# Attention matmuls in contiguous bursts, w1's loads behind w3's, and one tile of softmax sums with a scaling on ScalarE

## The chip, the core and the metric

One Trainium2 chip, one of its cores. The metric is the device time of one launch in microseconds (us). Engines: PE is TensorE (PEld its weight loads), DVE is VectorE, ACT is ScalarE, POOL is GpSimd, SP is SyncE, which here only issues DMAs. Each engine works through its own instructions in the order in which they were built; where one waits, all behind it on that engine wait too.

## The reference

Three stages. An attention of 4 batches x 8 heads x 576 positions x 64 (pooled by four, plus a local one in a band of 7), a product of weight matrices with a gate by `(x@w1)*(x@w2)`, and a mixture of eight experts that picks one expert per token.

```python
q_d, k_d, v_d = (t.reshape(B, H, Sd, 4, D).mean(axis=3) for t in (q, k, v))
out_up = np.repeat(sm_attn(q_d, k_d, v_d), 4, axis=2)
scores = np.where(np.abs(pos[:, None] - pos[None, :]) < 4, scale * q @ k.T, -1e9)
attn = np.exp(scores - scores.max(-1)); attn /= attn.sum(-1) + 1e-9
x = out_up + attn @ v                     # 2304 tokens x 512
x = ((x @ w1) * (x @ w2)) @ w3 @ w_out    # 512 -> 1024 -> 1024 -> 512
e = argmax(x @ w_gate); gate = softmax(x @ w_gate)[e] * sigmoid((x @ w_output_gate)[e])
out = gate * (relu(x @ e_w1[e]) @ e_w2[e])
```

## The kernel before

The weights w_out, w3, w1 and w2 arrive as 64-bit floats in tiles of 128x512 (512 KB). DVE makes 32-bit floats of each by three integer operations (`f64_bits`, L127 to L129); ACT then splits off a high part in a rounded format (the "hi" cast) and POOL or DVE takes the rest (the "lo" part). A product of full precision is three matmuls, hi x hi, hi x lo, lo x hi (`mm3`, L390 to L392); these are called the large matmuls below.

The program runs, in this order: the gate phase (w_out is converted, transposed and multiplied with the two gate matrices, L318 and L322); WC, the product w3 @ w_out (384 large matmuls of 256 or 272 columns, tiles `w3T`); then for six groups of 384 tokens G1, the products with w1 and w2 (192 matmuls of 384 columns per group, `g1_step`), and G2, the product with WC (144 matmuls of 256 or 272 columns per group, `g2_step`), with the routing of each group in between; then the eight experts. w1 and w2 are converted (`w_part`, two tiles per step) during G1 of group 0, whose step f needs the tiles of f.

Attention is cut into 16 units (a batch and two heads). A unit has five parts: `a_T` (pools q and k), `a_S1` (24 local score matmuls of 32x64, L191, here **S**; 3 pooled score matmuls of 96x144, L202, **D**; maxima, exponentials), `a_S2` (sums, reciprocals, the two scalings, L219 to L225), `a_V1` (transposes: DVE's of the local weights, PE's of the pooled ones, L245, **pT**) and `a_V2` (4 pooled value matmuls of 64x144, L256, and 12 local ones of 64x96, L260, together **V**). S writes 32 of the array's columns and V 64, by a position in the array; D, pT and the large matmuls are not placed so. The five parts of successive units are put between the steps of WC and G1 by tables of step numbers, under `tc.high_priority(offset=120)`: a list scheduler then sets the order on each engine by priorities, so that attention and large matmuls mix. Group g of G1 needs the units of its tokens: units 0 to 3 for group 0, 4 to 7 for group 1, and so on.

PSUM has eight banks: two each in `ps1` (tag g1) and `ps2` (tag g2), three in `psa` (attention and routing), one in `psc` (the temporary `cv` of `f64_bits`). SP issues all loads in one order; a load waits there until its buffer is free.

Of the kernel before, what the change touches and what calls it, by code (L numbers as in the profile page):

```python
# [48 lines left out]
def attention_moe_kernel(ctx: ExitStack, tc: tile.TileContext, q, k, vw_in, v4_in, w1, w2, w3, w_out,  # L49
# [52 lines left out]

    staged = {}

    def pieces(m, n):
        return (slice(0, 256), slice(256, 512)) if (m, n) == ("o", 0) else (slice(0, 512),)

    def f64_load(m, n):
        if m == "o":
            t = mt([P, 512], I64, "f64w", tag=f"W{n}")  # L110
            src = w_out[P * n:P * n + P, :]
        elif m == "3":
            t = mt([P, 512], I64, "f64w", tag=f"W{8 + n % 4}")
# [70 lines left out]
    def a_S1(u):  # L184
# [3 lines left out]
        sl = ps[:, 0:384].rearrange("p (b h k) -> p b h k", b=6, h=2)  # L188
        for g in range(24):
            b, j = divmod(g, 4)  # L190
            nc.tensor.matmul(sl[32 * j:32 * j + 32, b], qT[:, 24 * g:24 * g + 32], kz[:, :, 24 * g:24 * g + 32],  # L191
                             start=True, stop=True, tile_position=(0, 32 * j))
        sm = at([P, 6, 2, 32], F32, "sm", bufs=2)
# [6 lines left out]
        qf = qz.rearrange("p h n -> p (h n)")  # L200
        for qb in range(3):
            nc.tensor.matmul(sd[:, qb], qf[:, 96 * qb:96 * qb + 96], d["kd"], start=True, stop=True)  # L202
# [9 lines left out]
        d.update(sm=sm, ed=ed, zd=zd)  # L212

    def a_S2(u):
        d = st[u]
        sm, ed = d["sm"], d["ed"]
        su = at([P, 6, 2], F32, "su", bufs=2)
        sd = d["zd"]
        nc.vector.tensor_reduce(out=su, in_=sm, axis=AX.X, op=ALU.add)  # L219
        nc.vector.tensor_scalar(su, su, 1e-9, None, op0=ALU.add)  # L220
        nc.vector.reciprocal(su, su)
        nc.gpsimd.tensor_tensor(sm, sm, su.unsqueeze(3).to_broadcast([P, 6, 2, 32]), op=ALU.mult)
        nc.vector.tensor_scalar(sd, sd, 4.0, 4e-9, op0=ALU.mult, op1=ALU.add)
        nc.vector.reciprocal(sd, sd)
        nc.gpsimd.tensor_tensor(ed, ed, sd.unsqueeze(2).to_broadcast([96, 3, 144]), op=ALU.mult)  # L225
        v4 = d["v4"]
        vd = at([72, 2, 2, D], F32, "vd", bufs=2)
        vt = v4[:, :, 0:2]
        nc.gpsimd.tensor_tensor(vt, vt, v4[:, :, 2:4], op=ALU.add)
        nc.gpsimd.tensor_tensor(vd.rearrange("p k h d -> p k (h d)"), vt[:, :, 0], vt[:, :, 1], op=ALU.add)  # L230
        d.update(vd=vd)

    def a_V1(u):
# [8 lines left out]
        for kb in range(2):  # L242
            pv = psa.tile([P, 512], F32, name="at", tag="at")
            for qb in range(3):
                nc.tensor.transpose(pv[0:72, 96 * qb:96 * qb + 96], ed[:, qb, 72 * kb:72 * kb + 72], ident[0:96, 0:96])  # L245
            nc.scalar.copy(out=pt[:, kb], in_=pv[0:72, 0:288])
        d["pt"] = pt

    def a_V2(u):
# [3 lines left out]
        xl = [psa.tile([P, 512], F32, name="at", tag="at") for _ in range(2)]  # L253
        for kb in range(2):
            for h in range(2):
                nc.tensor.matmul(xl[0][64 * h:64 * h + 64, 288:432], vd[:, kb, h, :], pt[:, kb, 144 * h:144 * h + 144],  # L256
                                 start=(kb == 0), stop=(kb == 1))
        for c in range(6):
            for h in range(2):
                nc.tensor.matmul(xl[c // 3][64 * h:64 * h + 64, 96 * (c % 3):96 * (c % 3) + 96], vw[:, c, D * h:D * h + D],  # L260
                                 bd[:, 2 * c + h, :], start=True, stop=True)
        up = at([P, 144], F32, "up")
        nc.scalar.copy(out=up, in_=xl[0][:, 288:432])
        for a in range(2):
# [42 lines left out]
    def gate_step(f, gps, src):  # L307
        t = mt([P, DM], F32, "wf", tag=f"W{12 + f % 4}")
        for c in pieces("o", f):
            f64_bits(src[:, c], t[:, c].bitcast(U32))  # L310
        w = mt([P, NW + HN[1]], F32R, "wo", tag=f"h{f}")
# [47 lines left out]
    def w_part(m, f):  # L359
# [516 lines left out]
    for n in range(KF):  # L876
        if n == 1:
            nc.sync.dma_start(out=wg[:, :, 0:E], in_=w_gate.rearrange("(k p) e -> p k e", p=P))
            nc.sync.dma_start(out=wg[:, :, E:2 * E], in_=w_ogate.rearrange("(k p) e -> p k e", p=P))
        f64_load("o", n)  # L880
# [165 lines left out]
def _laid_out(inputs):  # L1046
# [51 lines left out]
```

## Time and profile before

| | |
|---|---|
| time, median of 3 runs | 777.54 us (775.76 to 778.25) |
| the profiled execution's own time | 771.75 us |
| its span, first to last instruction | 769.9 us |
| busy: PE, DVE, POOL, ACT | 96%, 57%, 42%, 36% |
| mean granted TensorE clock | 0.989 of full |

The profiled execution ended 5.8 us before the median of the timed runs, so differences are worked out on the profile and carried over to the median. A row of the timeline has the start in us, the length in us, the engine, the line, the operation, out<-in, the shapes and how many were merged; fp32 matmuls appear twice (x8 is four matmuls). The end of a matmul is modelled and includes the pipeline, so the time that one takes is read from start to start.

### The profile page before, as it was taken

What the parts mean: (1) busy time and instruction counts of PE and PEld (TensorE: products, weight loads), DVE (VectorE), ACT (ScalarE), POOL (GpSimd) and SP (SyncE); (2) the same over time, 40 slices, a digit from 0 to 9 for tenths busy, and PEclk for the clock granted to TensorE, in tenths of its full rate; (3) what the DMA queues carried; (4) which work ended last, traced back from release to release, by engine and by line L of the source; (5) the groups of instructions that cost most, each with busy time, mean ns of one, the idle gap of its engine ahead of it and who ended that gap; (6) DMA issues with size and microseconds to landing.
All of it is one profiled execution on the core that took longest, in us unless ns stands there. A gap on an engine that the chain in (4) does not pass through costs nothing.

```text
span 769.9 us, 14699 instructions
## 1 busy us (share of the span) xinstructions
PE 739.4 (96%) x5710; PEld 683.3 (89%) x5711; DVE 436.3 (57%) x940; ACT 279.6 (36%) x624; POOL 322.9 (42%) x306
## 2 busy tenths in 40 slices
PE   5789999999999999999999999989999999999995
PEld 3667987888978898899899999978999999999994
DVE  8977897962653254445324343455765566676731
ACT  3423534550233223323421212045443644544610
POOL 6744576852360125213201112035654656755611
PEclk9899999999999999999999999998999999999999
DMA  9994565542131313121110010256645447447301
GB/s 325 332 240 139 173 189 160 171 136 91 54 109 31 115 29 111 47 77 38 42 42 22 1 42 1 60 199 241 213 146 210 148 149 268 146 148 260 111 23 39
DMA packets 38264, 97.72 MB, mean 127 GB/s; under 512 B 6018, under 2 KB 12930, under 8 KB 38192
## 3 DMA queue, kind: packets, MB, share of 16 engines
q1 hardware_dynamic: 34768, 86.82, 35.1%
q0 software_dynamic: 3424, 9.93, 3.6%
q8 instruction: 46, 0.75, 0.4%
q14 instruction: 26, 0.21, 0.1%
HBM read 84.93 MB, written 12.29 MB: 126 GB/s over the span
## 4 chain that ended last, share of the span: by engine, by line
PE 86%; issue 5%; POOL 3%; DVE 3%; DMA 1%; ACT 1%; SPq 0%; POOLq 0%; ACTq 0%
PE g L390 24%; PE g L392 24%; PE g L391 23%; PE at L260 3%; PE at L191 3%; PE at L256 2%; PE at L202 2%; PE tr L686 1%; PE at L245 1%; PE tr L779 1%; POOL out_dram L769 1%; DMA early<-in_moe_w_dram 1%; PE g L322 1%; POOL W L713 1%; DVE wf L129 1%
## 5 line engine op out<-in xcount | busy, mean ns | idle before, releaser
L390 PE MATMUL g<-xh,W 128*128 128x384 f32 x384 | 133.8, 349 | 0.0
L392 PE MATMUL g<-xh,W 128*128 128x384 f32 x384 | 131.0, 342 | 0.0
L391 PE MATMUL g<-xl,W 128*128 128x384 f32 x384 | 130.8, 341 | 0.0
L713 DVE TENSOR_TENSOR W<-raw,W 128x1024 fp32r<-128x1024 f32 x32 | 87.9, 2780 | 32.2 <-ACT W L711 30.1
L713 POOL TENSOR_TENSOR W<-raw,W 128x1024 fp32r<-128x1024 f32 x29 | 82.8, 2879 | 37.0 <-ACT W L711 37.0
L390 PE MATMUL g<-xT,W 128*128 128x288 f32 (+6 forms) x256 | 82.2, 321 | 1.0 <-ACT xT L690 1.0
L391 PE MATMUL g<-xT,W 128*128 128x288 f32 (+6 forms) x256 | 80.2, 313 | 0.0
L392 PE MATMUL g<-xT,W 128*128 128x288 f32 (+6 forms) x256 | 80.0, 312 | 0.0
L423 POOL TENSOR_TENSOR h<-a,h 128x384 fp32r<-128x384 f32 x30 | 30.7, 1023 | 113.9 <-ACT h L421 113.7
L390 PEld LDWEIGHTS g<-xh,W 128*128 128x128 f32 x384 | 72.2, 188 | 3.2 <-issue 0.4
L392 PEld LDWEIGHTS g<-xh,W 128*128 128x128 f32 x384 | 72.1, 188 | 1.9 <-issue 0.4
L391 PEld LDWEIGHTS g<-xl,W 128*128 128x128 f32 x384 | 72.2, 188 | 1.5 <-issue 0.2
L390 PE MATMUL g<-wc,h 128*128 128x272 f32 (+1 forms) x240 | 70.2, 293 | 0.0
L391 PE MATMUL g<-wc,h 128*128 128x272 f32 (+1 forms) x240 | 70.0, 292 | 0.0
L390 PE MATMUL g<-h,W 128*128 128x288 f32 (+5 forms) x224 | 70.0, 312 | 0.0
L392 PE MATMUL g<-wc,h 128*128 128x272 f32 (+1 forms) x240 | 69.9, 292 | 0.0
L391 PE MATMUL g<-h,W 128*128 128x288 f32 (+5 forms) x224 | 68.1, 304 | 0.0
L392 PE MATMUL g<-h,W 128*128 128x288 f32 (+5 forms) x224 | 68.1, 304 | 0.0
L711 ACT CAST W<-raw 128x1024 fp32r<-128x1024 f32 x61 | 59.8, 1046 | 8.1 <-DMA raw<-in_moe_w_dram 4.3
L419 DVE TENSOR_TENSOR a<-g,a 128x384 f32<-128x384 f32 x48 | 26.7, 556 | 60.2 <-PE g L392 56.4
L739 ACT ACTIVATE h<-g 128x288 fp32r<-128x288 f32 (+6 forms) x64 | 27.9, 436 | 78.6 <-PE g L392 76.3
L390 PEld LDWEIGHTS g<-xT,W 128*128 128x128 f32 x256 | 49.1, 192 | 1.5 <-ACT xT L690 1.4
(255 smaller groups left out, 1721.8 us busy)
## 6 DMA issues: line engine op xcount, KB each, us to landing
raw<-in_moe_w_dram SPq DMA_DIRECT2D x61, 512.0 KB, 3.6
f64w<-in_moe_w_dram SPq DMA_DIRECT2D x16, 512.0 KB
f<-in_moe_w_dram SPq DMA_DIRECT2D x16, 512.0 KB, 6.5
vw<-in_vw_dram SPq DMA_DIRECT2D x16, 384.0 KB, 3.2
kc<-in_k_dram SPq DMA_DIRECT2D x16, 288.0 KB, 6.4
qT<-in_q_dram SPq DMA_DIRECT2D x16, 288.0 KB, 4.3
kz<-in_k_dram SPq DMA_DIRECT2D x32, 144.0 KB, 3.7
v<-in_v_dram SPq DMA_DIRECT2D x16, 288.0 KB
```

The source lines that it names most:

```text
L191: nc.tensor.matmul(sl[32 * j:32 * j + 32, b], qT[:, 24 * g:24 * g + 32], kz[:, :, 24 * g:24 * g + 32], start=True, stop=True, tile_positio ...
L202: nc.tensor.matmul(sd[:, qb], qf[:, 96 * qb:96 * qb + 96], d["kd"], start=True, stop=True)
L256: nc.tensor.matmul(xl[0][64 * h:64 * h + 64, 288:432], vd[:, kb, h, :], pt[:, kb, 144 * h:144 * h + 144], start=(kb == 0), stop=(kb == 1))
L260: nc.tensor.matmul(xl[c // 3][64 * h:64 * h + 64, 96 * (c % 3):96 * (c % 3) + 96], vw[:, c, D * h:D * h + D], bd[:, 2 * c + h, :], start=T ...
L390: nc.tensor.matmul(ps, whi, xhi, start=first, stop=False)
L391: nc.tensor.matmul(ps, whi, xlo, start=False, stop=False)
L392: return nc.tensor.matmul(ps, wlo, xhi, start=False, stop=last)
L419: nc.vector.tensor_tensor(a, pp[1][:, 0:G], a, op=ALU.mult)
L423: eng.tensor_tensor(lo, a, hi.bitcast(F32), op=ALU.subtract)
L711: nc.scalar.copy(out=hi, in_=t)
L713: ins = eng.tensor_tensor(lo, t, hi.bitcast(F32), op=ALU.subtract)
L739: return nc.scalar.activation(out=t[:, 0, 0:C], in_=ps[:, 0:C], func=AF.Relu), nc.vector.scalar_tensor_tensor(t[:, 1, 0:C], ps[:, 0:C], 0. ...
```

## The change

Six edits. (1) The PE instructions of S, D, pT and V are issued under a priority raised by a further 600, so that the scheduler puts them as soon as it counts their inputs as there, and together. (2) `psa` has four banks; `psc` is gone, and `cv` takes a bank of g1 (w_out and w3) or of g2 (w1 and w2). (3) The first four loads of w1 and w2 come behind the last load of w3 on SP. (4) Both softmaxes' sums lie in one tile of 128x15, with one addition of 1e-9 and one reciprocal for both; the factor 4 of the pooled one goes into the copy of V's result (0.25). (5) The pooled weights are scaled by three operations of ACT rather than one of POOL. (6) The two gate matrices are laid out in one row per partition by the host.

```diff
-    psa = actx.enter_context(tc.tile_pool(name="psa", bufs=3, space=PSUM))
-    psc = actx.enter_context(tc.tile_pool(name="psc", bufs=1, space=PSUM))
+    psa = actx.enter_context(tc.tile_pool(name="psa", bufs=4, space=PSUM))
...
-    def f64_bits(t, dst):
+    def f64_bits(t, dst, ps, tag):
...
-        c = psc.tile([P, 512], F32, name="cv", tag="cv").bitcast(U32)[:, 0:dst.shape[-1]]
+        c = ps.tile([P, 512], F32, name=tag, tag=tag).bitcast(U32)[:, 0:dst.shape[-1]]
...
+    sums = [at([P, 15], F32, f"sum{i}") for i in range(2)]
+    for t in sums:
+        nc.vector.memset(t, 1.0)
...
+    def burst():
+
+        return tc.high_priority(offset=600)
...
+        with burst():
+            for g in range(24):
+                b, j = divmod(g, 4)
+                nc.tensor.matmul(sl[32 * j:32 * j + 32, b], qT[:, 24 * g:24 * g + 32], kz[:, :, 24 * g:24 * g + 32],
+                                 start=True, stop=True, tile_position=(0, 32 * j))
...
-        zd = at([96, 3], F32, "zd", bufs=2)
+        zd = sums[u % 2][0:96, 12:15]
...
-        su = at([P, 6, 2], F32, "su", bufs=2)
-        sd = d["zd"]
+        sums_u = sums[u % 2]
+        su = sums_u[:, 0:12].rearrange("p (b h) -> p b h", b=6)
         nc.vector.tensor_reduce(out=su, in_=sm, axis=AX.X, op=ALU.add)
-        nc.vector.tensor_scalar(su, su, 1e-9, None, op0=ALU.add)
-        nc.vector.reciprocal(su, su)
+        nc.vector.tensor_scalar(sums_u, sums_u, 1e-9, None, op0=ALU.add)
+        nc.vector.reciprocal(sums_u, sums_u)
         nc.gpsimd.tensor_tensor(sm, sm, su.unsqueeze(3).to_broadcast([P, 6, 2, 32]), op=ALU.mult)
-        nc.vector.tensor_scalar(sd, sd, 4.0, 4e-9, op0=ALU.mult, op1=ALU.add)
-        nc.vector.reciprocal(sd, sd)
-        nc.gpsimd.tensor_tensor(ed, ed, sd.unsqueeze(2).to_broadcast([96, 3, 144]), op=ALU.mult)
+        for qb in range(3):
+            nc.scalar.activation(out=ed[:, qb], in_=ed[:, qb], func=AF.Copy, scale=sums_u[0:96, 12 + qb:13 + qb])
...
-        nc.scalar.copy(out=up, in_=xl[0][:, 288:432])
+        nc.scalar.mul(up, xl[0][:, 288:432], 0.25)
...
         if i == KF - 2:
-            ahead()
+            with tc.issue_after(f64_last[0].ins):
+                ahead()
```

The D, pT and V matmuls are put under `burst()` in the same way. How that moves the instructions shows at three places. The first is PE in G1 of group 1, where unit 8's V stands (`vd`, `vw` the values, `pt`, `bd` the weights, `xh`, `xl`, `W` the large matmuls'). Before:

```order
L391 MATMUL g1_2772<-xl_2382,W2_1618 128x384
L256 MATMUL at_2975<-pt_2759,vd_2630 64x144
L392 MATMUL g1_2772<-xh_2381,W6_1619 128x384
L256 MATMUL at_2975<-pt_2759,vd_2630 64x144
L390 MATMUL g1_2772<-xh_2381,W2_1618 128x384
L256 MATMUL at_2975<-pt_2759,vd_2630 64x144
L391 MATMUL g1_2772<-xl_2382,W2_1618 128x384
L256 MATMUL at_2975<-pt_2759,vd_2630 64x144
L392 MATMUL g1_2772<-xh_2381,W6_1619 128x384
```

And now (S and D of unit 10 just ahead of it):

```order
L199 MATMUL at_2828<-kz_108,qT0_109 32x64 x6
L211 MATMUL at_2858<-kd_2730,qz_112 96x144 x3
L199 MATMUL at_2828<-kz_108,qT0_109 32x64 x18
L266 MATMUL at_2955<-pt_2741,vd_2613 64x144 x4
L270 MATMUL at_2955<-bd_111,vw_2752 64x96 x6
L270 MATMUL at_2956<-bd_111,vw_2752 64x96 x6
L400 MATMUL g1_2796<-xh_2366,W3_1787 128x384
```

V's 16 matmuls, one by one between large ones before, stand in one piece; D has moved into the middle of S.

The second place is DVE around the end of WC (`f_...` are the loaded tiles of w1 and w2, `wc<-g` takes a finished half of WC out of its bank). Before:

```order
L355 TENSOR_TENSOR wc<-g_1065,wc 128x256
L127 TENSOR_SCALAR cv<-f_1138 128x512
L128 SCALAR_TENSOR_TENSOR cv<-f_1138,cv 128x512
L271 TENSOR_TENSOR xr<-at,up 128x288 x2
L129 SCALAR_TENSOR_TENSOR wf<-f_1138,cv 128x512
L127 TENSOR_SCALAR cv<-f_1140 128x512
```

Now:

```order
L365 TENSOR_TENSOR wc<-g_1295,wc 128x272
L127 TENSOR_SCALAR g_1352<-f_1132 128x512
L128 SCALAR_TENSOR_TENSOR g_1352<-f_1132,g_1352 128x512
L281 TENSOR_TENSOR xr<-at,up 128x192
L281 TENSOR_TENSOR xr<-at,up 128x96
L129 SCALAR_TENSOR_TENSOR wf<-f_1132,g_1352 128x512
```

The first tile of w1 was converted behind the sixth half of WC from the end (g_1065 is followed by five more), and is now converted behind the last but one (g_1295).

The third is SP, behind the first two loads of w3. Before:

```order
L169 DMA vw<-in_vw_dram 128x768
L119 DMA f_1138<-in_moe_w_dram 128x512
L119 DMA f_1140<-in_moe_w_dram 128x512
L119 DMA f_1142<-in_moe_w_dram 128x512
L153 DMA kc<-in_k_dram 128x576
L160 DMA kz<-in_k_dram 64x576 x2
```

Now:

```order
L176 DMA vw<-in_vw_dram 128x768
L160 DMA kc<-in_k_dram 128x576
L167 DMA kz<-in_k_dram 64x576 x2
L161 DMA qT_109<-in_q_dram 128x576
L160 DMA kc<-in_k_dram 128x576
L171 DMA v_549<-in_v_dram 72x1024
```

The loads of w1 and w2 have left this place; k and q of the next units stand there.

## Rows read from the trace of the kernel before

**Rows 1.** The page's first lines: span, then busy time of each engine.

```profile
span 769.9 us, 14699 instructions
```

**Rows 2.** Windows: stretch and its length, busy time by engine, clock, DMA share, GB/s.

```profile
0.00:28.70 28.70, 17.43 (x153) 12.69 (x154) 25.76 (x58) 12.45 (x27) 20.83 (x42) 1.00 0.94 335
28.70:101.10 72.40, 67.10 (x634) 57.67 (x638) 59.13 (x129) 30.82 (x83) 36.82 (x43) 0.95 0.71 202
101.10:168.20 67.10, 65.82 (x599) 56.27 (x598) 56.18 (x111) 33.03 (x88) 48.67 (x50) 1.00 0.55 167
168.20:242.30 74.10, 74.10 (x615) 63.73 (x614) 32.24 (x97) 21.72 (x62) 24.91 (x32) 1.00 0.26 78
242.30:318.20 75.90, 75.90 (x624) 66.61 (x623) 32.70 (x102) 24.14 (x67) 24.15 (x30) 1.00 0.27 79
318.20:400.00 81.80, 81.80 (x668) 76.39 (x667) 33.33 (x100) 25.32 (x68) 15.42 (x18) 1.00 0.14 42
```

**Rows 3.** Timeline of PE, 220 to 232 us: V between large matmuls one by one.

```profile
221.00 0.46 PE L256 MATMUL at<-pt,vd 72*64 72x144 f32 x2
221.39 0.45 PE L392 MATMUL g<-xh,W 128*128 128x384 f32 x1
...
231.47 0.34 PE L392 MATMUL g<-xh,W 128*128 128x384 f32 x1
```

**Rows 4.** Timeline of PE, 285 to 291 us: V in one piece, and pT.

```profile
285.27 0.71 PE L256 MATMUL at<-pt,vd 72*64 72x144 f32 x8
285.81 1.16 PE L260 MATMUL at<-bd,vw 128*64 128x96 f32 x24
...
287.19 0.34 PE L391 MATMUL g<-xl,W 128*128 128x384 f32 x1
287.36 0.34 PE L392 MATMUL g<-xh,W 128*128 128x384 f32 x1
...
290.46 0.66 PE L245 MATMUL at<-ident,ed 96*72 96x96 f32 x6
```

**Rows 5.** Timeline of PE, 218 to 221 us: S and D in one piece.

```profile
218.41 0.88 PE L191 MATMUL at<-kz,qT 128*32 128x64 f32 x48
219.21 0.98 PE L202 MATMUL at<-kd,qz 128*96 128x144 f32 x6
...
220.20 0.34 PE L391 MATMUL g<-xl,W 128*128 128x384 f32 x1
```

**Rows 6.** PE's groups by form, 168.2 to 400 us: xcount | busy us, mean ns.

```profile
L390 PE MATMUL g<-xh,W 128*128 128x384 f32 x200 | 70.2, 351 | 0.0
...
L390 PE MATMUL g<-wc,h 128*128 128x272 f32 x88 | 26.4, 300 | 0.0
...
L390 PE MATMUL g<-wc,h 128*128 128x256 f32 x82 | 24.0, 292 | 0.0
```

**Rows 7.** Groups of instructions, 0 to 168.2 us: the small operations of the softmaxes.

```profile
L210 ACT ACTIVATE ed<-at,md 96x144 f32<-96x144 f32 x24 | 8.8, 372 | 8.7 <-DVE md L206 8.7
...
L225 POOL TENSOR_TENSOR ed<-ed,zd 96x432 f32<-96x432 f32 x8 | 7.9, 993 | 4.2 <-DVE zd L224 4.2
...
L210 ACT ACTIVATION_READ_ACCUMULATOR ed<-at,md 96x1 f32 x24 | 4.7, 196 | 0.0
...
L223 DVE TENSOR_SCALAR zd<-zd 96x3 f32<-96x3 f32 x8 | 2.3, 289 | 0.0
...
L224 DVE RECIPROCAL zd<-zd 96x3 f32<-96x3 f32 x8 | 1.2, 156 | 0.0
```

**Rows 8.** Timeline of DVE, 96 to 99 us, and of PE, 116 us.

```profile
97.96 0.68 DVE L129 SCALAR_TENSOR_TENSOR wf<-f,cv 128x512 uint32<-128x512 uint32 x1
...
116.13 0.29 PE L392 MATMUL g<-wo,w3T 128*128 128x272 f32 x1
```

**Rows 9.** Timeline of PE, 50 us, and of POOL, 62 us: unit 2's D and its scaling.

```profile
50.09 0.41 PE L202 MATMUL at<-kd,qz 128*96 128x144 f32 x2
...
62.28 1.62 POOL L225 TENSOR_TENSOR ed<-ed,zd 96x432 f32<-96x432 f32 x1 [0.95 <-DVE zd L224]
```

More of the change, by code (lines that the diff above doesn't have):

```diff
@@ L103, in attention_moe_kernel @@
     staged = {}
+    f64_last = [None]
     def pieces(m, n):
@@ L188, in a_S1 @@
         sl = ps[:, 0:384].rearrange("p (b h k) -> p b h k", b=6, h=2)
[L189 to L192, printed above, removed]
+        with burst():
[3 more added lines that the diff above has]
+                                 start=True, stop=True, tile_position=(0, 32 * j))
         sm = at([P, 6, 2, 32], F32, "sm", bufs=2)
@@ L200, in a_S1 @@
         qf = qz.rearrange("p h n -> p (h n)")
-        for qb in range(3):
-            nc.tensor.matmul(sd[:, qb], qf[:, 96 * qb:96 * qb + 96], d["kd"], start=True, stop=True)
+        with burst():
+            for qb in range(3):
+                nc.tensor.matmul(sd[:, qb], qf[:, 96 * qb:96 * qb + 96], d["kd"], start=True, stop=True)
         ed = at([96, 3, 144], F32, "ed", bufs=2)
@@ L211, in a_S1 @@
                                  bias=md[:, qb:qb + 1], accum_out=zd[:, qb:qb + 1])
-        d.update(sm=sm, ed=ed, zd=zd)
+        d.update(sm=sm, ed=ed)
     def a_S2(u):
@@ L216, in a_S2 @@
         sm, ed = d["sm"], d["ed"]
-        su = at([P, 6, 2], F32, "su", bufs=2)
-        sd = d["zd"]
+        sums_u = sums[u % 2]
+        su = sums_u[:, 0:12].rearrange("p (b h) -> p b h", b=6)
         nc.vector.tensor_reduce(out=su, in_=sm, axis=AX.X, op=ALU.add)
-        nc.vector.tensor_scalar(su, su, 1e-9, None, op0=ALU.add)
-        nc.vector.reciprocal(su, su)
+        nc.vector.tensor_scalar(sums_u, sums_u, 1e-9, None, op0=ALU.add)
+        nc.vector.reciprocal(sums_u, sums_u)
         nc.gpsimd.tensor_tensor(sm, sm, su.unsqueeze(3).to_broadcast([P, 6, 2, 32]), op=ALU.mult)
-        nc.vector.tensor_scalar(sd, sd, 4.0, 4e-9, op0=ALU.mult, op1=ALU.add)
-        nc.vector.reciprocal(sd, sd)
-        nc.gpsimd.tensor_tensor(ed, ed, sd.unsqueeze(2).to_broadcast([96, 3, 144]), op=ALU.mult)
+        for qb in range(3):
+            nc.scalar.activation(out=ed[:, qb], in_=ed[:, qb], func=AF.Copy, scale=sums_u[0:96, 12 + qb:13 + qb])
         v4 = d["v4"]
@@ L243, in a_V1 @@
             pv = psa.tile([P, 512], F32, name="at", tag="at")
-            for qb in range(3):
-                nc.tensor.transpose(pv[0:72, 96 * qb:96 * qb + 96], ed[:, qb, 72 * kb:72 * kb + 72], ident[0:96, 0:96])
+            with burst():
+                for qb in range(3):
+                    nc.tensor.transpose(pv[0:72, 96 * qb:96 * qb + 96], ed[:, qb, 72 * kb:72 * kb + 72], ident[0:96, 0:96])
             nc.scalar.copy(out=pt[:, kb], in_=pv[0:72, 0:288])
@@ L253, in a_V2 @@
         xl = [psa.tile([P, 512], F32, name="at", tag="at") for _ in range(2)]
[L254 to L261, printed above, removed]
+        with burst():
+            for kb in range(2):
+                for h in range(2):
+                    nc.tensor.matmul(xl[0][64 * h:64 * h + 64, 288:432], vd[:, kb, h, :], pt[:, kb, 144 * h:144 * h + 144],
+                                     start=(kb == 0), stop=(kb == 1))
+            for c in range(6):
+                for h in range(2):
+                    nc.tensor.matmul(xl[c // 3][64 * h:64 * h + 64, 96 * (c % 3):96 * (c % 3) + 96], vw[:, c, D * h:D * h + D],
+                                     bd[:, 2 * c + h, :], start=True, stop=True)
         up = at([P, 144], F32, "up")
-        nc.scalar.copy(out=up, in_=xl[0][:, 288:432])
+        nc.scalar.mul(up, xl[0][:, 288:432], 0.25)
         for a in range(2):
@@ L877, in attention_moe_kernel @@
         if n == 1:
-            nc.sync.dma_start(out=wg[:, :, 0:E], in_=w_gate.rearrange("(k p) e -> p k e", p=P))
-            nc.sync.dma_start(out=wg[:, :, E:2 * E], in_=w_ogate.rearrange("(k p) e -> p k e", p=P))
+            nc.sync.dma_start(out=wg[:, :, 0:E], in_=w_gate.rearrange("p (k e) -> p k e", e=E))
+            nc.sync.dma_start(out=wg[:, :, E:2 * E], in_=w_ogate.rearrange("p (k e) -> p k e", e=E))
         f64_load("o", n)
@@ L1066, in _laid_out @@
         a[n] = _np.asarray(a[n]).reshape(KD, P, KF, P).transpose(2, 1, 0, 3).reshape(KF, P, 512)
+    for n in ("moe2_w_gate", "moe2_w_output_gate"):
+        a[n] = _np.asarray(a[n]).reshape(KD, P, E).transpose(1, 0, 2).reshape(P, KD * E)
     w = _np.asarray(a["moe2_w1"])
```

8 lines of the change are left out of this document (4 added, 4 removed).

## The prediction

> **What bounds the kernel now.** I read the page's head first, for the span [rows 1], then a table of windows by stage [rows 2], then the timeline of PE where attention mixes with large matmuls [rows 3 to 5]. The reader is to see two things in the windows. From 168.2 us on, PE is busy to the full (74.1 of 74.1, 75.9 of 75.9, 81.8 of 81.8) while DVE is at 32 to 33 us in each: here PE alone sets the end, and its time is a sum of what stands in its queue. Up to 168.2 us (the end of G1 of group 0) it is close: PE is busy 65.8 to 67.1 us of its stretches, but DVE is too, 25.76 of 28.7, 59.13 of 72.4 and 56.18 of 67.1, together 141.1 of 168.2 us. Every tile of w_out, w3, w1 and w2 passes through DVE there. So an edit on PE's queue is worth its full price behind 168.2 us, and before it only as far as DVE lets it.
>
> PE's "busy" hides a loss, and rows 3 and 4 show it. Two large matmuls of 384 columns in a row start 0.17 us apart (287.19 and 287.36 [rows 4]). One V in a single piece runs from 285.27 to 287.19, by when one large matmul (286.91 to 287.19) has run too: 1.92 less 0.17 is 1.75 us. The V that is mixed in one by one runs from 221.00 to 231.47, 10.47 us, with 15 large matmuls in it, which are worth 15 x 0.174 = 2.6 us: 7.86 us for the same V. Each of the 15 changes to and fro thus costs (7.86 - 1.75) / 15 = 0.41 us.
>
> **What the change does, part by part.** *Bursts behind 168.2 us.* First the floor of 168.2 to 400 us, 231.8 us long [rows 2]. Large matmuls: 3 x 200 of 384 columns, 3 x 88 of 272 and 3 x 82 of 256 [rows 6]. At 0.174 us, and in proportion to the columns 0.123 and 0.116 (an estimate), that is 104.4 + 32.5 + 28.5 = 165.4 us. Attention in single pieces: nine V at 1.75 = 15.8; eight S with D at 1.62 (218.41 to 220.20, less one large matmul [rows 5]) = 13.0; eight and a half pT at 0.66 at most [rows 4] = 5.6. The routing's 24 small matmuls I put at 2.5. The sum is 202.3, so 29.5 us are lost to changes. In the built order of before, PE goes 83 times from something else to S or V in this stretch, where 17 pieces (nine V, eight S with D) would need 17: 66 too many at 0.41 is 27 us, so count and loss agree.
>
> In the order of the changed kernel it goes there 31 times, for 16 pieces. The 15 beyond that are nearly all S again behind D: D now stands inside S (the first order fence). Before, no S stands right behind a D, so the price of that has no row. From below it is nothing, from above 0.41, as for a large matmul; I take 0.41, since a D uses the array unplaced, as a large matmul does. 15 x 0.41 = 6.2. The gain is 29.5 - 6.2 = 23.3; and one V (1.75) has moved ahead of 168.2, so this stretch gets shorter by 25.0. I take off 1.5 for places where a burst comes before its inputs do: **23.5 us**.
>
> A rule speaks against edit (1) here. The Trainium skill (TensorEngine Tiling (Array Packing), Key Properties) says that a change of tiling mode, not of tile alone, drains the engine. By that rule a burst with D in it is not one piece, as the 15 are counted above; a count of pieces alone, which lets them go free, would give 29.7 in place of 23.5. Rows 3 agree with the rule where large matmuls stand between; no row of before shows it for D inside S.
>
> *Up to the end of G1 of group 0.* The same work as before stands here, with V of the eighth unit in addition. PE's floor: in 28.7 to 168.2 us WC and G1 are 384 matmuls at about 0.12 and 192 at 0.174, 46 + 33 = 79 us. With five S and D, seven V and seven pT (8.1 + 12.3 + 4.6) and twelve changes too many (4.9) that is 109 us, and with two S, D and one V and pT that now stand ahead of WC (5.7) PE could end at 28.7 + 5.7 + 109 = 143 us. DVE's floor: edit (4) takes away 289 and 156 ns for eight units [rows 7], 3.6 us, so 137.5 us remain. In the busiest stretch of rows 2, the first, it is at 0.90; at that share it needs 153 us, at the 0.84 of the whole, 164. Two things hold it back. The 1e-9 is now added to both sums at once, so DVE waits for the pooled exponentials too, three of 372 + 196 ns on ACT [rows 7], 1.7 us per unit, and the conversions behind it wait along. And `cv` of w1 and w2 needs a bank of g2: four tiles had been converted when WC ended (the first at 97.96, WC's last matmul at 116.13 [rows 8]), now two; two tiles at 3 x 0.68 are 4 us behind WC, where G1 of group 0 waits for DVE with each step. I take 160 us for the end of this stage: **8 us** gained. Between the ends it can be 20 gained (148) or 4 lost (172).
>
> *Loads of w1 and w2 behind w3.* The first stretch moves 335 GB/s at a DMA share of 0.94 [rows 2], so 3 or 4 loads of 512 KB out of it bring k, q and w3 forward by some 1.5 us each. That comes off waits of DVE and is within the 8 us; w1's first tile is converted only at 96 to 99 us [rows 8]. If they came late, G1 of group 0 would wait for the first of them, at most the same 1.5 us each.
>
> *Edits with one answer.* The scaling moves from POOL (993 ns per unit [rows 7]) to ACT. The trace has no such operation; an ACT operation of this shape takes 372 ns, so three are 1.1 us, from nothing (where ACT waits anyway) to 1.7. ACT is busy 76 of the first 168.2 us and 22 to 25 in each later stretch [rows 2], so it hides there; if its queue is full, pT comes later by that much. It waits on the reciprocal, and w3's hi casts are queued behind it: that is in the range of the first stage. The fourth bank, 0.25 in the copy and the gate's layout cost and bring nothing that a row shows; the waits that a lack of a bank would have caused are covered by large matmuls, and would show as PE's idle time if that cover went.
>
> *Sum.* 8 + 23.5 = 31.5 us off the profiled execution's 771.75, to 740.25. Behind 400 us the order is the same and PE-bound or a chain behind PE, so it moves forward as a whole. The median of the runs is 777.54, 5.8 above the profiled one: the forecast for the median is **746.0 us**.
>
> **Rivals.** (a) *The first stage gives it back.* DVE's new wait for ACT costs eight times 1.7 = 13.6 us, and WC's end shifts 4: the stage ends at 172. For it: DVE is the second engine here, and its queue is in order. Against: the waits lie partly on work that is idle anyway. -4 + 23.5 = 19.5 gained: 758. The clock is a part of it: it was at 0.95 in 28.7 to 101.1 us, behind a stretch in which PE was busy only 17.43 of 28.7, and that is 3.6 us if it happens once more. The Trainium skill (TensorE: Matmul & The Clock Gate, What's actually happening) calls the throttled clock the default, which activity releases; the trace agrees with its 0.95 there and 1.00 where PE is full.
>
> (b) *The first stage comes down to near its floor*, 150, and no burst comes early: 18 + 25 = 43 gained, 734.5. For it: shorter queues of PE feed DVE's waits sooner. Against: DVE would need 0.92 all through.
>
> (c) *Slower: bursts hold PE in WC.* PE takes a burst in order. If pT stands in its queue before its weights are scaled, everything behind waits. Unit 2's D started at 50.09 and its scaling ended at 62.28 + 1.62 = 63.9 [rows 9]: 13.4 us in this stage, and now one more engine is in the chain. In the changed order the first units have little between D and pT (by the order and the prices above an estimated 4 us of PE's work for unit 0; for unit 4, 82 large matmuls, 10 us). The gain turns into a loss if the stage ends behind 168.2 + 23.5 = 191.7, four us per unit more than I forecast; at 5 us per unit over today's end it is 168.2 + 40, a loss of 16.5: 794. Against: PE shows few such waits in before although the same scheduler set its order.
>
> (d) *The switches aren't what costs:* the mixed V was slow for its own sake, waiting for `bd` or values, and bursts then wait as long in one place. 776, no change. Against: the step of rows 3 is the same at each of 15 places.
>
> **How the numbers follow.** The forecast has 0.50, (a) 0.24, (b) 0.14, (c) 0.08, (d) 0.04. The forecast's own range is 740 to 752 (the stage's end at 154 to 166). 733 to 764 takes in (b), (a) with one more lost clock stretch, and leaves out (c), (d) and some of the edges, about 0.2. About 0.3%, 2.3 us, is what a measurement can tell from no change: faster 0.88, same 0.04 (d), slower 0.08 (c).
>
> **What would show it.** Right: V's row in G1 of groups 1 to 3 always with x24 in one piece and PE's stretch from the end of G1(0) to the last attention some 25 us shorter; DVE nearer to 0.9 up to about 160 us; G1 of group 0 without attention in it, some 37 us long. A large matmul behind a D-S-D mix tells the price of the 15. Wrong: idle time of PE ahead of L254 (pT) or L199 (S) in WC (c); G1 of group 0 ending behind 168 us (a); a PE stretch behind it that is not shorter (d).

## The result and the profile after

The changed kernel takes **750.43 us** (median of 4 runs, 749.5 to 757.09) against 777.43 us for the kernel before in the same comparison: a ratio of 0.967, 95% interval [0.962, 0.973]. The forecast was 746.0 us, in a range of 733 to 764. The profiled execution took 751.11 us with a span of 749.4, 20.5 us less than the span of [rows 1].

The first view is the table of windows of the changed kernel. Each row has the stretch and its length, then busy time (and instructions) of PE, PEld, DVE, ACT and POOL, PE's granted clock, the DMA share and GB/s. The third row ends where G1 of group 0 ends, which was at 168.2 us in [rows 2].

```profile
0.00:28.70 28.70, 19.19 (x135) 13.20 (x137) 22.29 (x51) 9.95 (x17) 18.13 (x38) 1.00 0.94 310
28.70:101.10 72.40, 65.73 (x770) 57.85 (x770) 63.48 (x142) 40.69 (x121) 42.37 (x51) 0.91 0.72 232
101.10:171.05 69.95, 64.77 (x508) 59.91 (x508) 50.65 (x94) 34.50 (x85) 45.22 (x45) 0.95 0.49 156
171.05:248.00 76.95, 76.95 (x714) 72.39 (x714) 38.18 (x109) 31.56 (x92) 21.08 (x26) 1.00 0.28 86
248.00:325.00 77.00, 76.00 (x683) 72.47 (x682) 32.86 (x106) 24.92 (x71) 20.44 (x26) 1.00 0.24 70
325.00:380.35 55.35, 55.35 (x475) 52.07 (x474) 21.91 (x65) 21.06 (x55) 11.11 (x13) 1.00 0.13 37
```

Behind 171 us PE is full but for 1.0 us, as before, but more instructions fit: 714 in 76.95 us, 9.3 per us, where [rows 2] had 615 in 74.10, 8.3 per us. Ahead of it the clock is lower (0.91 and 0.95, before 0.95 and 1.00), DVE works less of the time (136.42 of 171.05 us, before 141.07 of 168.06, by the two tables below), and the stage ends later.

To place the gain, the program is cut at two points that both kernels pass: the end of G1 of group 0, and the end of the 86th matmul of the longest piece of G2 (96 matmuls in a row), the same matmul in every run, some 15 us ahead of the first expert. The same windows of the kernel before, with these cuts:

```profile
0.00:168.06 168.06, 150.21 (x1375) 126.49 (x1377) 141.07 (x296) 76.19 (x195) 106.32 (x133) 0.98 0.69 211
168.06:492.62 324.56, 324.56 (x2508) 299.18 (x2508) 132.42 (x422) 89.88 (x239) 76.89 (x92) 1.00 0.18 54
492.62:769.90 277.28, 264.60 (x1830) 257.63 (x1829) 162.81 (x224) 113.52 (x191) 139.65 (x81) 0.98 0.46 162
```

And of the kernel after:

```profile
0.00:171.05 171.05, 149.69 (x1410) 130.96 (x1412) 136.42 (x285) 85.14 (x222) 105.71 (x132) 0.94 0.67 214
171.05:472.97 301.92, 300.93 (x2473) 289.24 (x2473) 127.13 (x403) 96.14 (x259) 65.05 (x77) 1.00 0.18 54
472.97:749.40 276.43, 263.87 (x1831) 256.71 (x1829) 162.56 (x224) 113.67 (x191) 140.09 (x81) 0.98 0.46 162
```

The first stage is 2.99 us longer, the middle 22.64 us shorter, the rest (the end of G2 and the experts) 0.85 us shorter: 20.5 in all. The prediction had 8 shorter, 23.5 shorter and nothing.

In the middle stage a V in one piece now looks like this, with S ahead of it and a large matmul behind (PE's timeline after: start, us, engine, line, operation, what it writes and reads, tile, shape, count; compare [rows 3]):

```profile
222.18 0.75 PE L199 MATMUL at<-kz,qT 128*32 128x64 f32 x36
222.87 0.71 PE L266 MATMUL at<-pt,vd 72*64 72x144 f32 x8
223.41 1.16 PE L270 MATMUL at<-bd,vw 128*64 128x96 f32 x24
224.50 0.44 PE L400 MATMUL g<-xh,W 128*128 128x384 f32 x1
```

The prediction said that every V would be in one piece. Of the eight in this stage two are; the other six are cut once. And D stands inside its S:

```profile
206.03 0.31 PE L199 MATMUL at<-kz,qT 128*32 128x64 f32 x6
206.27 0.49 PE L211 MATMUL at<-kd,qz 128*96 128x144 f32 x2
206.68 0.30 PE L199 MATMUL at<-kz,qT 128*32 128x64 f32 x2
206.91 0.49 PE L211 MATMUL at<-kd,qz 128*96 128x144 f32 x2
207.33 0.30 PE L199 MATMUL at<-kz,qT 128*32 128x64 f32 x2
207.56 0.49 PE L211 MATMUL at<-kd,qz 128*96 128x144 f32 x2
207.97 0.76 PE L199 MATMUL at<-kz,qT 128*32 128x64 f32 x38
208.66 0.40 PE L583 MATMUL at<-rb 128*128 128x288 f32 x1
```

S and D take 2.63 us here, from 206.03 to 208.66.

In the first stage two things catch the eye on DVE. It stands for 3.33 us on ACT's copy of a transposed gate tile, and w3's first part goes through the last of its three steps only at 38.0 us (26.5 before); WC's first matmul starts at 45.39 us (28.67 before), and w1's first tile comes at 124.5 us (97.96 in [rows 8]).

```profile
24.91 0.70 DVE L127 TENSOR_SCALAR g<-f64w 128x512 uint32<-128x512 uint32 x1 [3.33 <-ACT wot L330]
...
38.01 0.66 DVE L129 SCALAR_TENSOR_TENSOR wf<-f64w,g 128x512 uint32<-128x512 uint32 x1
...
124.50 0.68 DVE L129 SCALAR_TENSOR_TENSOR wf<-f,g 128x512 uint32<-128x512 uint32 x1
```

The list of DVE's waits up to 171 us (us in total, times, longest) has one for ACT's exponentials ahead of the sums:

```profile
DVE sum L228 <- ACT sm L217: 5.9, 3, 3.4
...
DVE g L127 <- ACT wot L330: 3.3, 1, 3.3
```

It is not the one that the prediction spoke of. L228 adds up the local weights and waits for their exponentials (L217). The prediction's wait is that of the 1e-9 (L229) for the pooled exponentials (L219); up to 171 us DVE's list has none at L229, and over the whole span there is one, of 1.3 us. At the longest of the three waits at L228 the pooled exponentials are done over 4 us ahead of the local ones (the first two rows are ACT's, the others DVE's):

```profile
103.71 0.20 ACT L219 ACTIVATION_READ_ACCUMULATOR ed<-at,md 96x1 f32 x1
...
108.11 0.52 ACT L217 ACTIVATE sm<-sm 128x384 f32<-128x384 f32 x1
...
108.66 0.55 DVE L228 TENSOR_REDUCE sum<-sm 128x12 f32<-128x384 f32 x1 [3.38 <-ACT sm L217]
109.25 1.27 DVE L229 TENSOR_SCALAR sum<-sum 128x15 f32<-128x15 f32 x1
```

### The profile page after: what moved, and what is told of

It is laid out like the page before. It is cut to its first block, busy times and chain, and to the rows that moved or that the text cites. A ratio compares the mean times of both kernels' runs of the same rounds, so it can differ in the third digit from the quotient of the medians.

```text
span 749.4 us, 14701 instructions
## 1 busy us (share of the span) xinstructions
PE 714.5 (95%) x5710; PEld 676.9 (90%) x5711; DVE 426.1 (57%) x910; ACT 294.9 (39%) x672; POOL 310.9 (41%) x290
## 4 chain that ended last, share of the span: by engine, by line
PE 76%; issue 7%; DMA 5%; DVE 5%; POOL 4%; ACT 1%; SPq 1%; POOLq 0%; DVEq 0%; ACTq 0%
PE g L400 22%; PE g L402 21%; PE g L401 21%; PE at L211 2%; PE at L199 2%; PE at L270 2%; DMA v<-in_v_dram 2%; PE tr L696 1%; PE tr L789 1%; PE at L254 1%; PE at L266 1%; DMA vw<-in_vw_dram 1%; PE g L332 1%; DMA f64w<-in_moe_w_out_dram 1%; DMA early<-in_moe_w_dram 1%
## 5 line engine op out<-in xcount | busy, mean ns | idle before, releaser
L402 PEld LDWEIGHTS g<-xh,W 128*128 128x128 f32 x384 | 73.2, 191 | 3.3 <-POOL W L379 2.7
L400 PEld LDWEIGHTS g<-xh,W 128*128 128x128 f32 x384 | 73.2, 191 | 2.6 <-issue 0.8
L401 PE MATMUL g<-wc,h 128*128 128x272 f32 (+1 forms) x240 | 68.1, 284 | 0.0
L400 PE MATMUL g<-wc,h 128*128 128x272 f32 (+1 forms) x240 | 68.0, 284 | 0.0
L402 PE MATMUL g<-wc,h 128*128 128x272 f32 (+1 forms) x240 | 67.6, 284 | 0.0
```

The costliest lines, as they stand in the source:

```text
L400: nc.tensor.matmul(ps, whi, xhi, start=first, stop=False)
L401: nc.tensor.matmul(ps, whi, xlo, start=False, stop=False)
L402: return nc.tensor.matmul(ps, wlo, xhi, start=False, stop=last)
```

## The experiments

Open after this: whether changes of PE's use are what the middle stage gained (theory 1), and which part of the change turned 8 us of gain in the first stage into a loss of 3: the banks of the conversions (2), the merged sums (3), the order of the loads (4), or the clock (5). The table has, for each run, how often PE goes from something else to S or V behind G1 of group 0 in the built order, the end of the first stage, the length of the middle one (both from the profiled execution, cut as above) and the median time. The two stages are of one execution each, and that one lay between 2.3 us under (e5) and 3.4 above (e12) the median of its kernel, for before 5.7 under. The middle repeats to about 1 us between kernels with the same entries, so a first stage is known to a few us only, and the medians stand beside it where they say something else. The merged sums are always taken out together with ACT's scaling and the 0.25; the gate's layout is in every run.

| kernel | entries | first stage | middle | median us |
|---|---|---|---|---|
| before | 83 | 168.06 | 324.56 | 774 to 778 |
| after | 31 | 171.05 | 301.92 | 750.43 |
| e1 no bursts | 88 | 184.97 | 323.39 | 785.44 |
| e2 D behind S | 20 | 166.28 | 298.07 | 745.36 |
| e3 own bank | 34 | 160.95 | 302.59 | 744.18 |
| e4 sums apart | 29 | 170.91 | 300.23 | 749.35 |
| e5 own bank, w_out and w3 | 34 | 164.38 | 302.49 | 748.26 |
| e6 own bank, w1 and w2 | 34 | 173.91 | 302.26 | 751.73 |
| e7 = e3 + e2 | 18 | 161.82 | 295.94 | 737.30 |
| e8 = e3, loads early | 34 | 162.36 | 302.43 | 744.22 |
| e9 bursts and gate layout alone | 31 | 166.12 | 301.30 | 746.62 |
| e10 = e9 + e2 | 18 | 169.21 | 295.62 | 743.29 |
| e11 = e7, sums apart | 18 | 164.27 | 295.71 | 737.66 |
| e12 PE kept busy in two gaps | 31 | 172.53 | 302.14 | 750.45 |

**e1, the bursts taken away.**

```diff
-        return tc.high_priority(offset=600)
+        return tc.high_priority(offset=0)
```

> The changed kernel with the raised priority of the four pieces taken away (offset 0), all other edits kept. PE goes 88 times from something else to S or V behind G1 of group 0 instead of 31 times, and 63 times ahead of it instead of 32. Theory 1 (each change to and fro costs PE 0.37 to 0.41 us, and the bursts are what gained): the stretch from the end of G1 of group 0 (171.2 us in the changed kernel) to the end of the G2 block of group 3 (382.9) gets longer by 57 x 0.37 to 0.41 = 21 to 23 us; ahead of 171.2 us nothing to 12 us more, depending on whether VectorE covers it: 771 to 786 us. Rival (the changes of use cost nothing and some other edit, the loads or the banks, gained): that stretch stays at 212 us within 3, and the time at 748 to 754 us.

785.44 us, ratio to before 1.012 [1.006, 1.018]: without the bursts the other edits make the kernel 1.2% slower than it was. The windows of e1:

```profile
0.00:184.97 184.97, 162.66 (x1410) 134.14 (x1412) 140.36 (x285) 84.97 (x222) 102.66 (x131) 0.94 0.61 197
184.97:508.36 323.39, 323.39 (x2473) 297.80 (x2473) 129.32 (x403) 96.49 (x259) 65.39 (x78) 1.00 0.17 51
```

The middle has the same 2473 matmul rows as after and PE is full in both, yet it takes 323.39 in place of 301.92: 21.5 us for 57 changes, 0.377 us each. The entries to D and pT by themselves hardly differ between the two; what e1 adds are S and V alternating with large matmuls. The first stage is 13.9 us longer, so the bursts gained there too, more than the 12 at most that I gave them; other edits hid it.

**e2, D behind S.** S stays in one piece.

```diff
-                nc.tensor.matmul(sl[32 * j:32 * j + 32, b], ...
+                last_s = nc.tensor.matmul(sl[32 * j:32 * j + 32, b], ...
...
-        with burst():
+        with burst(), tc.issue_after(last_s.ins):
             for qb in range(3):
```

> The changed kernel with D's three matmuls held behind the last matmul of S, so that S stays in one piece; nothing else. Behind G1 of group 0 PE goes 20 times to S or V instead of 31, and ahead of it the pieces fall by about as much as D stood inside S (23 of S instead of 31 in all stages ahead). Theory 1 (D uses the array in another way than S, and each change costs 0.37 to 0.41 us): 11 x 0.37 to 0.41 = 4.1 to 4.5 us off the stretch behind G1 of group 0, with at most 2 us more ahead of it: 744 to 747 us. Rival (D inside S costs nothing beyond its own 0.5 us, the 2.63 us of the mixed S and D against 1.52 was a wait): 750 to 752 us. Rival 2 (D late makes the chain of the pooled softmax late, PE waits in the next pT): 752 to 756 us.

745.36 us. PE's timeline of e2, the same unit as in the mixed piece of after:

```profile
201.25 0.88 PE L199 MATMUL at<-kz,qT 128*32 128x64 f32 x48
202.06 0.98 PE L211 MATMUL at<-kd,qz 128*96 128x144 f32 x6
202.78 0.43 PE L400 MATMUL g<-xh,W 128*128 128x384 f32 x1
```

1.53 us in place of 2.63: three D inside S cost 1.10, 0.37 us each, about as much as a large matmul between. The middle is 3.85 us shorter for 11 changes (0.35 each); the first stage gives 4.8, where I had written 2 at most. By the medians the whole is 5.1, which leaves some 1 us to the first stage.

A straight line through the changed kernel and e1 to e11 gives 289.2 us + 0.39 us x entries for the middle, and each of them, e12 too, lies within 1.1 us of it (without e1, from 18 to 34 entries alone, the slope is 0.40). For before's 83 entries it gives 321.5; measured are 324.56, with one V of 1.75 more in it. So theory 1 holds: one price, near 0.39 us, over 18 to 88 entries.

**e3, the conversions' own bank** (attention back to three).

```diff
-    psa = actx.enter_context(tc.tile_pool(name="psa", bufs=4, space=PSUM))
+    psa = actx.enter_context(tc.tile_pool(name="psa", bufs=3, space=PSUM))
+    psc = actx.enter_context(tc.tile_pool(name="psc", bufs=1, space=PSUM))
...
-        c = ps.tile([P, 512], F32, name=tag, tag=tag).bitcast(U32)[:, 0:dst.shape[-1]]
+        c = psc.tile([P, 512], F32, name="cv", tag="cv").bitcast(U32)[:, 0:dst.shape[-1]]
```

> The changed kernel with the conversion's scratch bank given back (a bank of its own, and three for attention), all other edits kept. Theory 2 (the first stage became 3 us longer, not 8 shorter, because the conversions of w_out and w3 share the two G1 banks with PE's gate transposes and those of w1 and w2 wait for a G2 bank until WC is over): VectorE's 3.3 us at 24.9 us on ScalarE's copy is gone, the first w1 tile is converted at about 100 us instead of 124.5, and G1 of group 0 ends 5 to 9 us sooner, at 162 to 166 us: 742 to 746 us. If the loss comes from the merged sums instead (theory 3), it ends within 2 us of 171.2, at 749 to 753 us. If the fourth attention bank is what keeps bursts from waiting, attention's pieces wait for a bank and it is 753 to 758 us.

744.18 us, and the first stage ends at 160.95, even below theory 2's 162 to 166. In DVE's timeline of e3 the third step of a conversion stands at L130; w3's first part is finished 10.3 us sooner than after (27.75 against 38.01), w1's first tile 21.3 us sooner:

```profile
27.75 0.67 DVE L130 SCALAR_TENSOR_TENSOR wf<-f64w,cv 128x512 uint32<-128x512 uint32 x1
...
103.21 0.65 DVE L130 SCALAR_TENSOR_TENSOR wf<-f,cv 128x512 uint32<-128x512 uint32 x1
```

(The 26.7 us that e5's expectation gives for this is the step ahead of it.) WC's first matmul starts at 30.82 us in place of 45.39. The medians are 6.3 us apart, the first stages 10.1. The middle does not miss the fourth attention bank: 302.59 for 34 entries, on the line.

```profile
0.00:160.95 160.95, 144.36 (x1410) 125.36 (x1412) 138.02 (x285) 84.98 (x222) 106.54 (x132) 0.99 0.72 227
160.95:463.54 302.59, 301.70 (x2473) 289.89 (x2473) 128.41 (x403) 96.79 (x259) 64.38 (x77) 1.00 0.18 54
```

**e4, the sums apart again** (own sums, own reciprocals, GpSimd scales, no 0.25 in the copy).

```diff
-        nc.vector.tensor_scalar(sums_u, sums_u, 1e-9, None, op0=ALU.add)
-        nc.vector.reciprocal(sums_u, sums_u)
+        nc.vector.tensor_scalar(su, su, 1e-9, None, op0=ALU.add)
+        nc.vector.reciprocal(su, su)
...
-        for qb in range(3):
-            nc.scalar.activation(out=ed[:, qb], in_=ed[:, qb], func=AF.Copy, scale=sums_u[0:96, 12 + qb:13 + qb])
+        nc.vector.tensor_scalar(sd, sd, 4.0, 4e-9, op0=ALU.mult, op1=ALU.add)
+        nc.vector.reciprocal(sd, sd)
+        nc.gpsimd.tensor_tensor(ed, ed, sd.unsqueeze(2).to_broadcast([96, 3, 144]), op=ALU.mult)
```

> The changed kernel with the two softmaxes apart again: own sums and reciprocals, the pooled one scaled on GpSimd, no 0.25 in the copy; bursts, banks and loads kept. Theory 3 (VectorE's 1e-9 on both sums waits for ScalarE's pooled exponentials, 1.9 to 3.4 us where the trace shows it, and the conversions behind it wait along): G1 of group 0 ends 5 to 10 us sooner, at 161 to 166 us: 741 to 746 us. Theory 2 (the banks are what holds the first stage): within 2 us of 171.2, or later by up to 3.6 us for the small VectorE work that comes back: 749 to 755 us.

749.35 us; the first stage ends at 170.91, 0.14 sooner. Theory 3 falls: its wait of the 1e-9 isn't in the trace of after, and with the sums apart the stage ends where it did. The wait at L228 (L225 here) did get shorter: DVE's waits of e4 up to 171 us have 1.1 us left of the 5.9, but a longer wait for the bank stands beside it, and 1.7 us for the pooled exponentials at the pooled sums.

```profile
DVE g L127 <- ACT wot L328: 5.0, 1, 5.0
...
DVE su L225 <- ACT sm L214: 1.1, 3, 0.4
```

**e5 and e6, half of the bank each.** In e5 only w_out's and w3's conversions have their own bank, in e6 only w1's and w2's (with "g2" in the condition).

```diff
-        c = psc.tile([P, 512], F32, name="cv", tag="cv").bitcast(U32)...
+        c = (psc.tile([P, 512], F32, name="cv", tag="cv") if tag == "g1" else ps.tile([P, 512], F32, name=tag, tag=tag)).bitcast(U32)...
```

> The kernel of e3 with half of its edit: the conversions of w_out and w3 have their own bank, those of w1 and w2 go through the G2 bank as in the changed kernel. Of the 10.1 us that the bank gave ahead of G1 of group 0's end (171.05 to 160.95 us), theory 2a (w3 comes late: its first part is converted at 38.0 us, with the bank at 26.7 us, so WC starts its main work late) gives most to this half: the end at 161 to 164 us and 743 to 747 us, though w1's first tile is still converted only behind WC. Theory 2b (w1 and w2 behind WC are what costs, as the prediction had it with 4 us): the end at 167 to 171 us and 748 to 752 us.

> The other half: the conversions of w1 and w2 have their own bank, those of w_out and w3 share the two G1 banks with PE's gate transposes as in the changed kernel. Theory 2a: w3's first part is again converted at about 38 us and G1 of group 0 ends at 168 to 171 us: 748 to 752 us. Theory 2b: w1's first tile is converted well ahead of WC's end and G1 of group 0 ends at 161 to 165 us: 742 to 746 us. If both halves count, each gives some 4 to 6 us.

748.26 and 751.73 us; the first stage ends at 164.38, just above theory 2a's bounds, and at 173.91, above all of them. So the half for w_out and w3 gives 6.7 of e3's 10.1 us; the one for w1 and w2 gives the other 3.4, but only on top of it. Alone (e6) it finishes w1's first tile at 102 us and gains nothing; w3 is late there, its first part comes at 37.56 us. By the medians the shares are others: e5 is 2.2 us below the changed kernel and e3 another 4.1 below e5, since e5's profiled execution was its fastest. So both halves count once the first is there, and how the 6 to 10 us divide is not settled. e6's clock was also low from 45 to 101 us (0.85), and what of its 2.9 us loss that made isn't separated.

**e7, both that helped: own bank and D behind S.**

> e3's and e2's edits together: the conversions' own bank and D behind S. Behind G1 of group 0 the changes of use that D makes inside S go, 3.85 us in e2; ahead of it e2 gave 4.8 us and e3 10.1 us. If these are of different causes (theory 1 for D, theory 2 for the bank), the sum is 10.1 + 4.8 + 3.85 = 18.8 us off the changed kernel: 732 to 736 us. If ahead of 171 us they cover each other (VectorE is what holds that stage once PE is not), it is 10.1 + 3.85 = 14 off: 736 to 741 us.

737.30 us, 0.950 [0.946, 0.954] of before: 13 us below the changed kernel.

```profile
0.00:161.82 161.82, 138.19 (x1410) 124.15 (x1412) 140.22 (x285) 84.25 (x222) 105.20 (x132) 0.97 0.74 226
161.82:457.76 295.94, 295.58 (x2473) 288.00 (x2473) 130.88 (x403) 95.94 (x259) 64.78 (x77) 1.00 0.18 55
```

The middle gets e2's gain and more (6.65 us for 16 entries). The first stage gets none of e2's 4.8: PE has 6 us less to do there than in e3 (138.19 against 144.36), while DVE is at 0.87 of the time, 140.22 of 161.82. That fits a stage that DVE now holds near 161 us; no run shows it.

**e8, e9, e10 and e11, the other edits.** e8 is e3 with w1's and w2's loads free to go early:

```diff
-            with tc.issue_after(f64_last[0].ins):
-                ahead()
+            ahead()
```

> e3 with the loads of w1 and w2 free to go early, as in the kernel before. Theory 4 (the loads behind w3's bring k, q and w3 forward; the prediction put 1.5 us to each of 3 or 4 loads): G1 of group 0 ends 2 to 5 us later than in e3's 161 us: 746 to 750 us. Rival (their order does nothing once the conversions have a bank): within 2 us of e3, 742 to 746 us.

744.22 us, e3's time: next to e3 the order of the loads does nothing. e9 keeps of the whole change the bursts and the gate's layout alone.

> The kernel before with the bursts and the gate's layout alone: banks, loads and softmax sums as before. If the bursts are the whole gain and the other edits bring nothing (e3, e4 and e8 each gave the time back or left it), G1 of group 0 ends at 159 to 164 us and the stretch behind it, with 31 changes to S or V as in the changed kernel, takes 300 to 303 us: 741 to 746 us, faster than the changed kernel by 5 to 9 us. If the merged sums or the late loads gain something that the shared banks hid in e4 and e8, it is 746 to 752 us.

746.62 us, just inside the second range, and 3.8 us below the changed kernel: the other edits together lose. The first stage, at 166.12, is 3.8 us longer than e8's, which differs by the merged sums and what goes with them alone (2.4 by the medians), so where the bank is free these may help. e10 adds D behind S to e9, e11 takes the merged sums out of e7.

> e9 with D behind S: 18 changes to S or V behind G1 of group 0 in place of 31, at 0.38 us 5 us less than e9: 736 to 740 us, the same as e7 within 3 us if the loads and the sums bring nothing. If the late loads and the merged sums do help once the conversions have their bank, e7 stays ahead by 3 to 6 us.

> e7 with the softmax sums apart as before: 18 changes behind G1 of group 0, as in e7. The merged sums save VectorE 0.445 us per unit and GpSimd 1 us, but make VectorE wait for ScalarE; in e4 that was 0.1 us ahead of G1 of group 0's end. If it stays covered with the bank given back: within 2 us of e7, 735 to 739 us. If the wait counts now (VectorE has 28 us of work per 34 us in this stage): 3 to 6 us faster, 731 to 734 us. If the saved VectorE work counts: 3 us slower, 740 to 742 us.

743.29 and 737.66 us. Both middles are 5.6 to 5.7 below e9's, as 13 entries at 0.39 say (5.1), but e10's first stage came out 3.1 us longer than e9's: a miss. e10 is 6.0 us behind e7, as its expectation had it for loads and sums that help. e11 ties with e7 (its runs span 732.06 to 742.39). What sums and loads are worth between -1 and +6 us is not settled: e8 against e3 gives nothing for the loads, e10 against e11, which differ by them alone, 5.6, and each edit moves the order of the whole first stage.

**e12, PE kept busy.** In the changed kernel PE's clock falls about the end of gaps, and the row of 28.7 to 45.4 us reads 0.69:

```profile
28.70:45.40 16.70, 13.74 (x165) 10.26 (x164) 12.05 (x34) 9.04 (x32) 11.41 (x16) 0.69 0.56 169
```

e12 fills two gaps with transposes of the identity into unused columns.

```diff
+    def fill(ps, n):
+        for _ in range(n):
+            nc.tensor.transpose(ps[:, 384:512], ident, ident)
...
+        if f == KF - 2:
+            fill(gps, 8)
...
+        fill(ps, 12)
```

> The changed kernel with 20 transposes of the identity into unused columns of two PSUM tiles, put where PE waits in the changed kernel: 8 behind the seventh gate tile (PE idle from 29.6 to 30.8 us) and 12 behind the transposes of the gate sums (36.4 to 38.2 us). In the changed kernel's profile the granted clock falls to half about 1 to 2 us behind each of these two gaps and stays there for some 10.4 us in all between 28.7 and 45.4 us (0.69). Theory 5 (these gaps bring the clock down, and the lower clock costs PE up to half of that stretch): the clock of 28.7 to 45.4 us is at 0.9 or above, and G1 of group 0 ends 2 to 5 us sooner, at 166 to 169 us: 746 to 749 us. Rival A (the clock stays up but PE only waits longer, since VectorE's order and the banks set this stage): clock at 0.9 or above, the end within 1.5 us of 171, 749 to 752 us. Rival B (the fall of the clock has nothing to do with these gaps): clock at 0.8 or below again, the end at 171 to 173 us, 750 to 753 us.

750.45 us. The same window of e12:

```profile
28.70:45.40 16.70, 12.88 (x199) 10.77 (x198) 11.97 (x27) 9.34 (x33) 12.09 (x18) 1.00 0.55 161
```

The clock stayed at 1.00, and DVE got through as much as in the changed kernel (11.97 us of work against 12.05). WC's first matmul started 3.4 us sooner (42.00), yet the first stage ended 1.5 us later, at 172.53, the border of rival A. So rival A, in this one profile and in the median alike: with the clock up in these 16.7 us the stage ends no sooner. That PE doesn't count at all in the first stage doesn't follow: e1, with 13 us more of PE's work there, ended 13.9 us later.

## Why the prediction was right, and where it was not

**Bursts behind 168.2 us: right.** 23.5 us were forecast, 22.64 came: 52 entries fewer at 0.39 and the one V make 22.0. The price of 0.41 per change was taken from one V [rows 3, 4]; over the kernels of the table it is 0.39, and 0.37 for D inside S, where I had only the bounds nothing and 0.41. By the rule of the Trainium skill (TensorEngine Tiling (Array Packing), Key Properties) that a change of tiling mode drains the engine, D inside S is no single piece. e2's rows agree, with 1.10 us for three; they show the price, not that it is a drain.

**Up to the end of G1 of group 0: wrong by 11 us in the profiled executions**, 8 gained forecast, 2.99 lost. The terms, one by one. DVE's work was right (137.5 forecast, 136.42 in the window). The bank of w1 and w2 at 4 us was right in size (3.4 by the profiles of e3 and e5, 4.1 by their medians). The wait of the merged sums, 1.7 us per unit, did not come: no wait stands at L229 in this stage. What the trace has is 5.9 us at the local sum, and e4, where 1.1 of it is left, ends the stage 0.1 us sooner. G1 of group 0 is free of attention, as forecast, and takes 40.5 us from its first matmul to its end, where 37 were forecast.

The step that failed is another. "The fourth bank ... cost and bring nothing that a row shows" was written of attention's side, and for the gate and w3, whose conversions now take turns in G1's two banks with PE's transposes, I had put nothing. That is 6.7 us by e5's profile and 2.2 by its median; both halves together are 10.1 and 6.3. That it works by DVE's wait for ACT's copy and by a later place of w3 in DVE's queue is read from the two timelines; the two were not separated. With the bank given back the stage ends at 160.95; my 160, less the 4 us for the bank, would be 156. So of the 11 us some 6 are the bank's (10.1 in place of 4) and 5 lie elsewhere: DVE came to 0.86 of that time (138.02 of 160.95 in e3), 156 would have needed 0.88, and less work for PE didn't raise it beyond 0.87 (e7). What holds DVE there is not settled.

Whether the stage lost or gained is less sure than the profiles look. The medians are 27.0 us apart, the profiled executions 20.5. If the other 6.5 us lie in the first stage, which no trace shows, it gained 3.5 us by the medians, and the forecast of 8 was 4.5 too much.

**Rival (a)** named the end of the stage, 172 us, for the wrong reason: its eight waits for ACT don't stand in the trace, and the clock, where e12 gave it back, was worth nothing. Rival (d), that the switches aren't what costs, is refuted by e1, and (c), bursts that hold PE, by a middle stage in which PE is idle for 1.0 of 301.92 us. In the first stage bursts do hold PE now and then (a V waits 2.0 us for its values ahead of G1 of group 0), but e1 shows that without them it is 13.9 us longer.

**The loads** were put at 1.5 us each within the first stage; e8 against e3 shows nothing, e11 against e10 5.6 us in all, so their size stays open.

**The level.** By the sum the profiled time would have been 740.25; 751.11 came, about 11.0 of the difference from the first stage, 0.9 from the middle, less 0.85 from the experts. The forecast for the median was nearer (746.0 against 750.43) by luck: I added the 5.8 us by which the profiled execution of before lay under its median, while that of after lay 0.7 above its own.

## What to carry to other kernels

Where PE is full and small placed matmuls stand between large ones, count the changes in its queue and multiply: the price came out the same over 18 to 88 entries, and a piece of another kind inside a burst counts like any other. When a scratch buffer is given up to share another's banks, follow every user of those banks in order, not only the one that gets the freed bank: the loss was on DVE and ahead of G1, where the bank given to attention had nothing to do. And undo the edits of a bundle one at a time, and then in pairs: here one edit gave the gain, one cost 6 us by the medians, and D behind S, which was not among them, was worth another 5. Compare medians too: a stage read from one execution of each kernel was off by several us.

## What the runs showed of the hardware that was not expected

In the changed kernel PE's granted clock fell to half (1.2 GHz) at 31.3 and 38.1 us, at the end of these two waits, and came back later,

```profile
30.84 0.31 PE L199 MATMUL at<-kz,qT 128*32 128x64 f32 x6 [1.19 <-DMA kz<-in_k_dram]
...
38.20 0.44 PE L199 MATMUL at<-kz,qT 128*32 128x64 f32 x6 [1.77 <-DVE wo L344]
```

and three times more up to 171 us, each time behind a gap of 1.2 to 2.0 us, but not behind every such gap. In e12 a gap of the same kind is left behind the eight transposes, and the clock stayed at 2.4 GHz:

```profile
32.21 0.31 PE L199 MATMUL at<-kz,qT 128*32 128x64 f32 x6 [1.67 <-DMA kz<-in_k_dram]
```

So the gap alone doesn't tell it. What the lower clock of 28.7 to 45.4 us cost didn't reach the time in e12.

The 1.00 of the first window, here and in [rows 2], says less than it seems: the trace holds no record of the clock ahead of 24.5 us (15.6 in before). The same group of eight matmuls of the gate phase takes 1.91 us ahead of that and 1.06 behind it, so PE ran at about half its speed up to there, and the mean clocks don't count it:

```profile
21.24 1.91 PE L332 MATMUL g<-wot,wg 128*32 128x128 f32 x8 [0.73 <-ACT wot L330]
...
25.49 1.06 PE L332 MATMUL g<-wot,wg 128*32 128x128 f32 x8
```

Over 36 executions of the kernel before, run beside the experiments, the times lie between 770.5 and 782.3 us and the mean clock between 0.976 and 0.990: the 16 at a clock below 0.985 have a median of 779.4 us, the other 20 of 774.0. Two versions some 5 us apart need several runs each.
